# Memory rows handed over in two parts, Q and K passes interleaved, and layernorm rows transposed by DMA in a two-layer attention kernel

## The chip, the cores and the metric

The kernel runs on one core of one Trainium2 chip, as one launch. The metric is device time in microseconds, smaller is better. Before the change three runs took 2330.82, 2334.03 and 2334.85 us; the median is 2334.03. The profiled execution has a span of 2335.8 us.

## The reference

Four layers are applied in turn to x of 2048 tokens by 640 features: A, B, A, B. Each adds its output to x, and each gets the layernorm of x as input. A is a linear and softmax attention with 32 heads of 20 in four segments; the change leaves it alone. B is a recurrence over 64 segments of 32 tokens:

```
mem = mem0                                    # 8 memory rows of 640
for s in range(64):
    h = concat(mem, xs)                       # 8 + 32 rows
    q, k, v = h @ Wq, h @ Wk, h @ Wv          # 32 heads of 128
    p = softmax(mask(q k^T / sqrt(128)))
    o = (p v) @ Wo
    mem, out[s] = o[:8], o[8:]
```

The memory rows of a step are the first eight output rows of the step before. So a step can begin to project its memory only when the output projection of the step before is done.

## The kernel before

Everything is in bfloat16 with float32 sums. Only layer B is touched. The order of the instructions on TensorE (PE), ScalarE (ACT), VectorE (DVE) and GpSimd (POOL) is the order of the program text, held by explicit order edges; the DMAs that SP issues are not in those edges.

**A step of layer B** (the loop from line 933, `i4` = s mod 4, `T` = s // 4) works on 32 new columns: 8 memory rows and 24 tokens of the next segment, all in the transposed tile `hT[s]` of 128 partitions by 5 chunks by 56 columns. Columns 24 to 32 are the memory. The last 8 tokens of each of four segments (a group T) are collected in `hx[T]` by `tail_cols` (line 776), a POOL copy, and are projected by "tail" units, which serve as filling work of the steps i4 = 1, 2, 3 of the group before. In i4 = 0 the filling work is the output projection of the group's 32 deferred rows (`b_OPSd`).

**A pass** (`thin_parts`, line 750) is five parts, one for each chunk c of 128 features. A part is four matmuls of 32 output rows by 512 columns that share the array; it adds into one PSUM buffer of a pool of three. The tile names are `b_Qa`, `b_Ka`, `b_Qb`, `b_Kb` (Q and K of heads 0 to 15 and 16 to 31) and `b_V`. When a Q or K pass ends (`QKPass`, line 1002), DVE turns the 32x32 blocks of its sums (`turn`, into `b_TQ`, two buffers), DVE casts the memory columns into `QT[s]` or `KT[s]`, and POOL casts the other 24 for step s + 1.

**The order of a step** on PE: Qa, Ka, Qb, two parts of Kb, `scores(0)`, three parts of Kb, then, if there are any, the transposes of `ln_tr`; one part of V0, `sums(0)`, four parts of V0, `scores(1)`, three parts of V1, `values(0)`, two parts of V1, `sums(1)`, half of the output projection `b_OPS`, filling work, `values(1)`, more filling work, the other half of `b_OPS`, and by `fill(9)` all the filling work that is left.

**The hand-over** (lines 1157 to 1162): when `b_OPS` is done, DVE turns all 320 columns of it into `b_TM` by one stream transpose, and two adds of 64 partitions by 40 elements write the memory columns of `hT[s + 1]`. PE meanwhile works on what `fill(9)` issued; then its first weight load of Qa waits for those columns.

**The layernorm for layer B** goes by groups of 128 tokens. In the steps with i4 = 2, `ln_norm` and `ln_apply` make the normed rows `b_xn` (one buffer, DVE). In the next step, `ln_tr` (line 710) transposes its five blocks on PE into PSUM, and ACT copies them to `b_xnTg`, a tile of two buffers. Its readers are POOL copies: `tail_cols` one step later, and `alloc_h` from three steps later on. At a layer's start group 1 is made just before the loop and transposed in step 0; there SP also loads the second part of the output weights `b_wo` (line 915).

**SP's queue** in a step carries the loads of the residual rows (`b_XO`, line 1120, `b_XOd`, line 929), the stores of the results (lines 1172 and 1185) and, every four steps, the load of the next 128 rows (`b_xt`, line 698).

Of the kernel before, what the change touches and what calls it, by code (L numbers as in the profile page):

```python
# [19 lines left out]
BF16 = mybir.dt.bfloat16  # L20
ACT = mybir.ActivationFunctionType
ALU = mybir.AluOpType
# [7 lines left out]
NCH = 5  # L30
# [630 lines left out]
def layer_B(nc, nc_raw, tc, C, W, br, outer, wo_src, x_src, xb_src, x_dst, general, nsteps=64, out_bf16=False):  # L661
# [3 lines left out]
    NT = nsteps // 4  # L665
    with ExitStack() as ctx:
# [38 lines left out]
        def ln_apply(g):  # L705
            xt, (mv, rstd) = ln_n[g]
            xn = ln_n[g] = wk.tile([128, D], BF16, name="b_xn", tag="xn")
            layernorm_apply(nc, xt[:], xn[:], mv, rstd)

        def ln_tr(g):  # L710
            xn = ln_n.pop(g)
            tps = pot.tile([128, NCH, 128], BF16, name="b_lntps", tag="ot")
            for c in range(NCH):
                nc.tensor.transpose(tps[:, c, :], xn[:, 128 * c:128 * c + 128], C.identb[:])
            xg = wk2.tile([128, NCH, 128], BF16, name="b_xnTg")
            nc.scalar.copy(xg[:], tps[:])
            xnT_g[g] = xg

        def xcols(s, a, b):
# [4 lines left out]
        hT, QT, KT = {}, {}, {}  # L724
# [51 lines left out]
        def tail_cols(T):  # L776
            if T not in hx:
                hx[T] = wk.tile([128, NCH, 32], BF16, name="b_hx", tag="hx")
                v = xnT_g[T][:].rearrange("p c (i t) -> p c i t", t=32)[:, :, :, 24:32]
                nc.gpsimd.tensor_copy(hx[T][:].rearrange("p c (i t) -> p c i t", t=8), v)  # L780
            return lambda c: hx[T][:, c, :]
# [135 lines left out]
        pot = ctx.enter_context(tc.tile_pool(name="b_pot", bufs=2, reuse_waits="tile", space=PSUM))  # L917
# [15 lines left out]
        for s in range(nsteps):  # L933
            last = (s == nsteps - 1)
            T, i4 = divmod(s, 4)
# [20 lines left out]
            def fill(us):  # L956

                while queue and us > 0.1:
                    cost, f = queue.pop(0)
                    f()  # L960
                    us -= cost
# [56 lines left out]
            def qk(Wt, name, b, dst):  # L1018

                QKPass(Wt, name, b, dst).run()  # L1020
# [36 lines left out]
            def normalise(b):  # L1057

                R = (wk if general else sm).tile([128, 4, 40], F32, name="b_R", tag="R")
                flat = R[:].rearrange("p r c -> p (r c)")  # L1060
                nc.scalar.activation(out=flat, in_=SP[b][:, 256:416], func=ACT.Ln)
                nc.scalar.activation(out=flat, in_=flat, func=ACT.Exp, scale=-1.0)
                nc.vector.tensor_tensor(out=PT[:, b, :, 16:56], in0=PT[:, b, :, 16:56], in1=R[:], op=ALU.mult)
                nc.gpsimd.tensor_tensor(out=PT[:, b, :, 0:16], in0=PT[:, b, :, 0:16], in1=R[:, :, 24:40], op=ALU.mult)
                if not general:
                    nc.gpsimd.tensor_tensor(out=Rtot[:], in0=Rtot[:], in1=R[:], op=ALU.add)
# [13 lines left out]
            def take(eng, b, jp):  # L1080
                h = 16 * b + 8 * jp
                evac(eng, OTsb[:, h:h + 8, :].rearrange("p (j r) c -> p j (r c)", j=2), OTL[b, jp][:, :, 0:160])
# [11 lines left out]
                    if not self.parts:  # L1094
                        evac(("act", "dve")[self.b], Vsb[:, self.b, :], self.ps[:])

            qk(W.wq, "b_Qa", 0, QT)
            qk(W.wk, "b_Ka", 0, KT)
            qk(W.wq, "b_Qb", 1, QT)
            if general:  # L1100
                row_max(0)
# [3 lines left out]
            K1.run(3)  # L1105
            while xn_pending:
                ln_tr(xn_pending.pop(0))
            if i4 == 0 and T + 1 < NT:
                tail_cols(T + 1)
            V0 = VPass(0)  # L1110
            V0.run(1)
            sums(0)
# [17 lines left out]
            take("act", 0, 0)  # L1130
            take("act", 0, 1)
            normalise(1)
            if g_need < NT:
                ln_apply(g_need)
                xn_pending.append(g_need)
            if i4 != 3:
                tails_to_seg(s + 1)
            op = OPass(lambda h: OTsb[:, h, 0:32], HORDER, "b_OPS", po, "op")
# [9 lines left out]
            ops = op.ps  # L1148
# [7 lines left out]
                deferred[T] = OPass(lambda h, t_=OTd: t_[:, h, :], HORDER, "b_OPSd")  # L1156
            if not last:
                TM = wk.tile([128, 10, 32], F32, name="b_TM", tag="TM")
                nc.vector.transpose(out=TM[:].rearrange("p g t -> p (g t)"), in_=ops[:])
                for hf in range(2):  # L1160
                    nc.vector.tensor_tensor(out=hT[s + 1][64 * hf:64 * hf + 64, :, 24:32], in0=TM[0:64, hf:10:2, 24:32],
                                            in1=TM[64:128, hf:10:2, 24:32], op=ALU.add)
            fill(9)
            flush()
            if not last and i4 == 3:
# [36 lines left out]
def full_kernel(tc, A_x, A_wq, A_wk, A_wv, A_wo, A_beta, B_x, B_mem0, B_Wq, B_Wk, B_Wv, B_Wo, B_seg_len, out, layers="ABAB"):  # L1202
    nc = tc.nc
    with ExitStack() as ctx:
# [14 lines left out]
        def run(general):  # L1219
            nc.scalar.preload_act_table_set("natural_log_exp_and_others")  # L1220
            nl = len(layers)
            assert layers == "AB" * (nl // 2)
            onc = _OrdNC(tc, nc, engines=ORDER_ENGINES)
            for li in range(0, nl, 2):
                lastl = (li == nl - 2)
                first = li == 0 and not general
                with ExitStack() as bridge, ExitStack() as outer:
                    outer.bridge = bridge
                    br = layer_A(onc, nc, tc, C, WA, A_wv, A_wo, xin if li == 0 else X, X, Xb, li == 0, general, outer, mem0,
                                 prep=prep if first else None, prefetch=loads if first else ())  # L1230
                    layer_B(onc, nc, tc, C, WB, br, outer, wo_src, X, Xb, xout if lastl else X, general, out_bf16=lastl)
# [61 lines left out]
```

## Time and profile before

| what | value |
|---|---|
| span of the profiled execution | 2335.8 us |
| PE busy | 2225.5 us, 95% |
| DVE busy | 1576.3 us, 67% |
| POOL busy | 1036.7 us, 44% |
| ACT busy | 950.3 us, 41% |
| transpose b_TM, 128x320 | 126 times, 517 ns |
| add into b_hT, 64x40 | 252 times, 195 ns at least |
| transposes b_lntps, 128x128 | 150 times, 219 ns (median) |
| copy b_xnTg | 30 times, 692 ns |
| copy b_hx | 30 times, 407 ns (median) |

A row of the timeline gives the start in us from the span's start, the duration in us, the engine, the operation with the tile written and the tiles read, the shape, the count of merged instructions, and in brackets the idle time of the engine just before with what ended it. PEld is the weight load, which runs ahead of the matmuls. A row of the waits gives the total in us, the number of waits and the longest. A row of the chain gives start and duration of a piece of the path that ended last. The matmuls' ends are modelled, and four of a part run side by side, so lengths are better taken from starts. The page's first line of each engine counts busy time, its share of the span, and instructions.

Layer B takes two stretches of the span, from about 317 to 1150 us and from about 1476 to 2326 us. A step of it lasts 12.95 to 13.5 us.

### The profile page before, as it was taken

How to read it: one execution, taken by the hardware profiler on the slowest of the kernel's cores; microseconds unless marked ns; L12 is line 12 of the kernel's file. 1: busy time of each engine (PE TensorE's matmuls, PEld its weight loads, DVE VectorE, ACT ScalarE, POOL GpSimd, SP SyncE). 2: the span in 40 equal slices, each digit the busy share in tenths (PEclk: the TensorE clock that was granted, in tenths of full speed). 3: DMA queues.
4: the chain of work that ended last, by engine and by line, in shares of the span. 5: the costliest groups of instructions: out<-in, count | busy, mean ns of one | idle time of the engine just before them, and what ended most of it. 6: DMA issues, size and time to landing. Idle time of an engine off the chain costs nothing.

```text
span 2335.8 us, 122651 instructions
## 1 busy us (share of the span) xinstructions
PE 2225.5 (95%) x54988; PEld 1238.1 (53%) x54988; DVE 1576.3 (67%) x3618; ACT 950.3 (41%) x2207; POOL 1036.7 (44%) x2475
## 2 busy tenths in 40 slices
PE   6999989999999999999889899899999999999997
PEld 3444545555555555555545445455555555555554
DVE  5777746666666666666657777566666666666664
ACT  5776823323232333323257767223333233323332
POOL 3344534444444444444324445344444444444442
PEclk9999989999999999999989999999999999999998
DMA  6555540000000000000133334300000000000000
GB/s 165 146 148 152 161 142 20 21 18 20 18 19 19 20 21 20 21 15 17 31 104 115 108 117 127 124 18 15 17 15 17 16 18 16 17 18 16 14 12 14
DMA packets 90649, 123.38 MB, mean 53 GB/s; under 512 B 16496, under 2 KB 80000, under 8 KB 88192
## 3 DMA queue, kind: packets, MB, share of 16 engines
q1 hardware_dynamic: 87648, 111.84, 16.9%
q8 instruction: 431, 7.06, 1.3%
q10 hardware_dynamic: 2464, 3.61, 0.6%
q14 instruction: 106, 0.87, 0.1%
HBM read 89.17 MB, written 26.21 MB: 49 GB/s over the span
## 4 chain that ended last, share of the span: by engine, by line
PE 80%; DVE 10%; ACT 5%; issue 2%; DMA 2%; POOL 0%; SPq 0%; DVEq 0%; ACTq 0%; POOLq 0%
PE b_OPS L85 14%; PE b_V L85 13%; PE b_Qa L85 7%; PE b_tail L85 7%; PE b_Kb L85 6%; PE b_Ka L85 6%; PE b_Qb L85 6%; PE b_SP L85 4%; PE a_PP L85 4%; ACT a_PT L85 4%; PE b_OTL L85 3%; PE b_OPSd L85 3%; PE a_S L85 2%; PE a_pv L85 2%; DVE a_qk L85 2%
## 5 line engine op out<-in xcount | busy, mean ns | idle before, releaser
L85 PEld LDWEIGHTS <-b_hT 128*32 128x32 bf16 x15120 | 369.8, 96 | 334.7 <-DVE b_hT L85 66.6
L85 ACT ACTIVATE b_PT<-b_SP 128x224 bf16<-128x224 f32 x256 | 92.2, 360 | 784.6 <-DVE b_TQ L85 740.2
L85 PE MATMUL b_V<-b_wv,b_hT 128*32 128x512 bf16 x5040 | 355.8, 381 | 0.0
L85 ACT ACTIVATE a_PT<-a_S 128x768 bf16<-128x768 f32 (+1 forms) x384 | 326.7, 892 | 62.4 <-PE a_S L85 56.2
L85 PE MATMUL b_OPS<-b_wo,b_OTsb 128*32 128x320 bf16 x8192 | 329.9, 303 | 6.5 <-DVE b_OTsb L85 5.2
L85 PEld LDWEIGHTS <-b_OTsb 128*32 128x32 bf16 x8192 | 197.3, 97 | 115.4 <-DVE b_OTsb L85 49.4
L85 POOL CAST b_QT<-b_TQ 128x384 bf16<-128x384 f32 x254 | 142.7, 562 | 240.9 <-DVE b_TQ L85 240.9
L85 ACT CAST b_OTsb<-b_OTL 128x320 bf16<-128x320 f32 x384 | 151.0, 428 | 232.3 <-PE b_OTL L85 204.7
L85 POOL CAST b_KT<-b_TQ 128x384 bf16<-128x384 f32 x254 | 142.9, 563 | 175.5 <-DVE b_TQ L85 174.3
L85 POOL TENSOR_TENSOR b_PT<-b_PT,b_R 128x64 bf16<-128x64 bf16 x256 | 105.6, 412 | 222.1 <-ACT b_R L85 197.4
L85 POOL TENSOR_SCALAR_AFFINE_SELECT a_PT<-a_PT 128x256 bf16<-128x256 bf16 x256 | 109.0, 427 | 172.6 <-ACT a_PT L85 161.0
L85 PE MATMUL b_Kb<-b_wk,b_hT 128*32 128x512 bf16 x2520 | 182.5, 380 | 0.0
L85 PE MATMUL b_Qa<-b_wq,b_hT 128*32 128x512 bf16 x2520 | 162.3, 387 | 13.7 <-DVE b_hT L85 7.2
L85 PE MATMUL b_Ka<-b_wk,b_hT 128*32 128x512 bf16 x2520 | 160.0, 383 | 0.0
L85 PE MATMUL b_Qb<-b_wq,b_hT 128*32 128x512 bf16 x2520 | 158.1, 380 | 0.0
L85 PE MATMUL a_PP<-a_xnT,a_wt 128*128 128x512 bf16 x560 | 146.1, 394 | 5.2 <-DVE a_um L85 1.5
L85 DVE STREAM_TRANSPOSE b_TM<-b_OPS 128x320 f32<-128x320 f32 x126 | 65.1, 517 | 118.2 <-PE b_OPS L85 118.2
L85 PE MATMUL a_S<-a_qk 32*128 32x512 bf16 (+3 forms) x1024 | 137.3, 308 | 7.8 <-ACT a_PT L85 6.5
L85 DVE CAST b_Vsb<-b_V 128x512 bf16<-128x512 f32 x128 | 88.5, 692 | 74.6 <-PE b_SP L85 43.9
L85 DVE TENSOR_TENSOR b_PT<-b_PT,b_R 128x160 bf16<-128x160 bf16 x256 | 103.8, 405 | 48.3 <-ACT b_R L85 29.2
L85 DVE STREAM_TRANSPOSE b_TQ<-b_Qa 128x512 f32<-128x512 f32 x128 | 91.7, 717 | 65.7 <-PE b_Qa L85 45.4
L85 DVE CAST b_OTsb<-b_OTL 128x320 bf16<-128x320 f32 x128 | 62.9, 492 | 106.0 <-PE b_OTL L85 105.2
(165 smaller groups left out, 4270.0 us busy)
## 6 DMA issues: line engine op xcount, KB each, us to landing
a_wt<-a_wpad SPq DMA_DIRECT2D x112, 160.0 KB
b_XO<-xres SPq DMA_DIRECT2D x256, 30.0 KB
a_wvo<-in_A_wo_dram SPq DMA_DIRECT2D x8, 800.0 KB
b_wq<-in_B_Wq_dram SPq DMA_DIRECT2D x20, 256.0 KB
b_wk<-in_B_Wk_dram SPq DMA_DIRECT2D x20, 256.0 KB
xres<-a_xo SPq DMA_DIRECT2D x16, 320.0 KB
xres_bf<-a_xb SPq DMA_DIRECT2D x32, 160.0 KB
b_wv<-in_B_Wv_dram SPq DMA_DIRECT2D x20, 256.0 KB
```

The costliest lines, as they stand in the source:

```text
L85: r = f(*a, **k)
```

## The change

There are four edits.

1. The hand-over is made in two parts: DVE turns the first 128 columns of `b_OPS` (chunks 0 and 1) and adds them into `hT[s + 1]`, then the other 192 (chunks 2 to 4).
2. The passes Qa and Ka are interleaved: two parts of Q, two of K, three of Q, three of K. So chunks 2 to 4 are first read by the fifth part.
3. `tail_cols(T + 1)`, in steps with i4 = 0, moves from behind the Kb pass to behind `normalise(1)`.
4. `ln_tr` issues one transposing DMA on SP's queue, from `b_xn` to `b_xnTg` in SBUF, in the place of five PE transposes, their PSUM tile and the ACT copy.

```diff
         def ln_tr(g):
             xn = ln_n.pop(g)
-            tps = pot.tile([128, NCH, 128], BF16, name="b_lntps", tag="ot")
-            for c in range(NCH):
-                nc.tensor.transpose(tps[:, c, :], xn[:, 128 * c:128 * c + 128], C.identb[:])
             xg = wk2.tile([128, NCH, 128], BF16, name="b_xnTg")
-            nc.scalar.copy(xg[:], tps[:])
+            nc.sync.dma_start(xg[:], xn[:], transpose=True)
             xnT_g[g] = xg
...
-            qk(W.wq, "b_Qa", 0, QT)
-            qk(W.wk, "b_Ka", 0, KT)
+            Q0, K0 = QKPass(W.wq, "b_Qa", 0, QT), QKPass(W.wk, "b_Ka", 0, KT)
+            Q0.run(2)
+            K0.run(2)
+            Q0.run(3)
+            K0.run(3)
             qk(W.wq, "b_Qb", 1, QT)
...
             while xn_pending:
                 ln_tr(xn_pending.pop(0))
-            if i4 == 0 and T + 1 < NT:
-                tail_cols(T + 1)
             V0 = VPass(0)
...
             normalise(1)
+            if i4 == 0 and T + 1 < NT:
+                tail_cols(T + 1)
             if g_need < NT:
...
                 TM = wk.tile([128, 10, 32], F32, name="b_TM", tag="TM")
-                nc.vector.transpose(out=TM[:].rearrange("p g t -> p (g t)"), in_=ops[:])
-                for hf in range(2):
-                    nc.vector.tensor_tensor(out=hT[s + 1][64 * hf:64 * hf + 64, :, 24:32], in0=TM[0:64, hf:10:2, 24:32],
-                                            in1=TM[64:128, hf:10:2, 24:32], op=ALU.add)
+                for c0, c1 in ((0, 2), (2, NCH)):
+                    nc.vector.transpose(out=TM[:, 2 * c0:2 * c1].rearrange("p g t -> p (g t)"), in_=ops[:, 64 * c0:64 * c1])
+                    for hf in range(2):
+                        nc.vector.tensor_tensor(out=hT[s + 1][64 * hf:64 * hf + 64, c0:c1, 24:32], in0=TM[0:64, 2 * c0 + hf:2 * c1:2, 24:32],
+                                                in1=TM[64:128, 2 * c0 + hf:2 * c1:2, 24:32], op=ALU.add)
```

## The prediction

> **What bounds the kernel now.** I read the page's busy shares and its chain first.
>
> ```profile
> PE 2225.5 (95%) x54988; PEld 1238.1 (53%) x54988; DVE 1576.3 (67%) x3618; ACT 950.3 (41%) x2207; POOL 1036.7 (44%) x2475
> PE 80%; DVE 10%; ACT 5%; issue 2%; DMA 2%; POOL 0%; SPq 0%; DVEq 0%; ACTq 0%; POOLq 0%
> ```
>
> TensorE is the bound; DVE has a tenth of the chain, and in layer B that tenth is chiefly the hand-over between steps. So only what shortens TensorE's queue, or a wait of TensorE, is worth time. Second, the waits of TensorE's weight loads:
>
> ```profile
> PEld L85 <- DVE b_hT L85: 66.6, 126, 1.7
> PEld L85 <- DVE b_xn L85: 11.9, 28, 0.4
> ```
>
> Each of the 126 hand-overs waits for the memory rows in b_hT. Part of it is only the loader running ahead of the array, so third, the timeline at one hand-over (i4 = 2 to 3):
>
> ```profile
> 729.12 1.25 PE L85 MATMUL b_tail<-b_wq,b_hx 128*32 128x512 bf16 x20
> 729.34 0.52 DVE L85 STREAM_TRANSPOSE b_TM<-b_OPS 128x320 f32<-128x320 f32 x1 [0.44 <-PE b_OPS L85]
> 729.89 0.53 DVE L85 TENSOR_TENSOR b_hT<-b_TM 64x40 bf16<-64x40 f32 x2
> 730.46 0.72 DVE L85 STREAM_TRANSPOSE b_TQ<-b_tail 128x512 f32<-128x512 f32 x1
> 730.48 2.06 PEld L85 LDWEIGHTS <-b_hT 128*32 128x32 bf16 x44 [0.61 <-DVE b_hT L85]
> 731.87 0.72 DVE L85 STREAM_TRANSPOSE b_TQ<-b_Qa 128x512 f32<-128x512 f32 x1 [0.69 <-POOL b_QTt L85]
> ```
>
> Call x the start of the b_TM transpose (729.34). In the chain, 20 such matmuls are spaced 1.08 us, 0.2155 us per part of four. The tail fill would therefore let Qa start at 729.12 + 1.08 = 730.20, x + 0.86; it starts at 730.48, x + 1.14. The array loses 0.28 us, not 0.61. By the same sum the hand-over after i4 = 1 loses 0.18 (fill from 716.16, Qa at 717.42), that after i4 = 3 loses 0.28, and that after i4 = 0, filled by nine b_OPSd parts of 0.135 from 703.21, loses 0.05. A group of four steps loses 0.79 us.
>
> Fourth, the chain through a step with the layernorm transposes and one without:
>
> ```profile
> 721.56 0.67 PE b_Kb L85 x12
> 722.24 0.22 PE b_V L85 x4
> ...
> 734.63 0.67 PE b_Kb L85 x12
> 735.30 0.39 PE b_lntps L85 x5
> 735.68 0.33 PE b_V L85 x4
> ```
>
> The five transposes take 0.39 us on the bounding engine, and the first V part after them 0.11 more.
>
> **What the Trainium skill says.** "TensorE: Matmul & The Clock Gate", Back-to-back issue gap, gives N/2.4 + 2.5 ns for warm matmuls: 215.8 ns at 512 columns. The trace agrees (0.2155). "VectorE: DVE Perf Modes", The three transpose paths, prices a crossbar DMA transpose of a 128x128 bf16 block at 1309 ns; no transfer of this trace is one. "DMA: Bandwidth & Descriptors", Queues, rings and completion order, says that descriptors are consumed in ring order; the trace cannot show it, but it decides where a transpose behind a large load lands.
>
> **Rows turned in two parts.** DVE transposes of 512 and 320 columns last 717 and 517 ns: 1.04 ns a column and 184 fixed. So 128 columns cost 0.317 and 192 cost 0.384 us. The two adds last 195 ns at 40 elements, some 0.17 at 16 and 0.18 at 24. The first half is ready at x + 0.317 + 0.03 + 0.17 + 0.03 + 0.17 + 0.05 (semaphore) = x + 0.77. After i4 = 2 and 3 POOL's b_OTdef copy overlaps and the adds take 0.53 instead of 0.43, so I take x + 0.87. The array is free at x + 0.85, so the hand-overs gain 0.05, 0.17, 0.25 and 0.25: 0.72 a group. The second half follows after 0.414 + 0.42, at x + 1.60 to 1.75.
>
> **Q and K interleaved.** Q0 and K0 run two parts each before Q0 needs chunk 2: 4 x 0.2155 = 0.86 us after a start at x + 0.86, so x + 1.72. The second half is just in time; its price lies between 0 and 0.1 a step, and I take 0. The price elsewhere is that the Q pass ends two parts later, counting from its start t0 (6 x 0.2155 + 0.38 = 1.67 us), and K only three parts after it. DVE must turn Q and K back to back. What this takes is seen at the start of the layer:
>
> ```profile
> 317.81 0.71 DVE L85 STREAM_TRANSPOSE b_TQ<-b_Qa 128x512 f32<-128x512 f32 x1
> 318.55 0.23 DVE L85 CAST b_QT<-b_TQ 128x128 bf16<-128x128 f32 x1
> 318.69 0.71 DVE L85 STREAM_TRANSPOSE b_TQ<-b_Ka 128x512 f32<-128x512 f32 x1
> 319.44 0.23 DVE L85 CAST b_KT<-b_TQ 128x128 bf16<-128x128 f32 x1
> ```
>
> A turn and its cast recur every 0.88 us. So Q's turn starts at t0 + 1.67 + 0.12 = 1.79, K's at 2.67, and K's cast ends at 3.65 (before: Qa at 704.46, cast end at 707.91, 3.45). scores(0) loads K at 708.14, t0 + 3.68. With 0.05 of semaphore the stall is 0.02 to 0.06 us; if cast and turn did not overlap (0.98 apart) it would be 0.12. I take 0.04 a step, 0.16 a group. Queued behind the longer b_TM chain (DVE ends at x + 1.6 instead of 0.98) are the second tail turn or add_out: 0.72 or 1.01, done by x + 2.6, while Q's turn is wanted at x + 2.65. PSUM slots hold: scores(0) takes Ka's, free at t0 + 3.39.
>
> Sum: 0.72 - 0.16 = 0.56 a group, times 15 filled groups in each of two layers: 16.8 us. The six hand-overs without fill (start and end of the layers) gain about 0.25 each, 1.5. Together 18.
>
> **Layernorm transposes by DMA.** Removed: 30 times five TensorE transposes. A step with them lasts 742.83 - 729.34 = 13.49 us, one without 12.95, of which 0.10 is the larger loss at the hand-over it begins with: 0.44, times 30 = 13 us. The ACT copy (692 ns x30) also goes, at no gain: ACT is busy for 41%. Added: 30 transposes on SP's queue. b_xn is ready at 726.94; its first reader is the b_hx copy of the next i4 = 0 step, now behind normalise(1) at about 753.7. That is 26 us, against 5 x 1.31 = 6.5 us (an estimate from the skill's price) and SP behind it: the next store waits for DVE until 738.29 anyway. So it costs nothing in the steady state; the work that hides it is a whole step of matmuls. Bounds: 0 to the rival below. At a layer's start the transpose shares SP with the b_wo loads (issued at 318.53), on which layer two's chain waits 12.94 us. Behind them it lands when DMA falls quiet near 331, plus some us, and POOL has until about 336 (its cast of step 1's Q starts at 338.11, and the b_QT, c_tot, b_OTdef and b_hT copies between take 1.5); ahead of them it delays them by its length. Between 0 and 6.5 us a layer; I take 0.5, 1 in all.
>
> **tail_cols moved.** One POOL copy of 0.40 us, x30, passes values(0)'s b_PT multiply; the chain shows no loss there (OTL follows V at 750.98 as elsewhere) and POOL's next piece, the b_QT copy, is needed 7 us later. Nothing. It issues no DMA.
>
> **Total:** 18 + 13 - 1 = 30 us off the profiled span of 2335.8. The unprofiled runs are 2330.8 to 2334.9, so 2334 - 30 = 2304.
>
> **Rivals.**
> Hand-over paid back: the second half comes 0.1 late in every step (12 us of 120 filled hand-overs), or the K turn costs 0.12 instead of 0.04 (10 us), or both. Speaks for it: both margins are below 0.1 us. One of them leaves 18 to 20 us, both leave 8: 2314 to 2326, most likely 2316.
> No early release: if TensorE's first weight load waits for all four adds, it starts at x + 1.60 instead of x + 1.03 to 1.14, 0.5 x 126 = 63 slower, less 13: 2384. Against it: scores(0) reads half of QT (708.14) before the cast into its other half (708.76), so waits go by region.
> The other side, by DMA: at both layer starts, with DMA share over 1, TensorE stops for an unnamed reason, in the chain
>
> ```profile
> 323.65 3.19 issue
> ```
>
> (2.65 us in layer two), which looks like starved instruction supply. If each transpose did that, 30 x 3 = 90 us less 31 gained: near 2393. It decides from 31/30, 1.0 us, a transpose. Against it: the 160 KB b_xt load at 726.96 leaves no gap on TensorE.
> No change: half of the hand-over gain is lost and layer starts cost 6 us each with some stalls; about 2332.
>
> **How the numbers follow.** Forecast 0.56 (2290 to 2313); paid back 0.22; no early release 0.06; starved by DMA 0.09; no change 0.07. Within 0.2% (4.7 us, about what a measurement here can tell) is no change. Faster: 0.56 + 0.22 less a little = 0.77; slower 0.06 + 0.09 + 0.01 = 0.16. Range 2288 to 2331: the first two cases.
>
> **What would show it.** Right: b_TM as x252 at about 0.32 and 0.38 us; the b_hT wait down from 66.6 to some 45 us or less; b_Ka starting 0.43 after b_Qa; no b_lntps, i4 = 3 steps at 13.0 us; b_hx never waiting for a DMA. Wrong: new waits of scores(0) on b_KT above 0.06 a step, of b_Qa on the second add, "issue" gaps on TensorE beside the transposes, or POOL stopped at b_hx early in a layer.

## The result and the profile after

| kernel | median us | range | runs | ratio to before (95% interval) |
|---|---|---|---|---|
| before | 2333.35 | 2330.82 to 2334.85 | 4 | |
| changed | 2313.88 | 2309.95 to 2317.14 | 4 | 0.9917 [0.9899, 0.9935] |

The change makes the kernel 0.8% faster, 19.5 us where 30 were forecast. The profiled span fell from 2335.8 to 2315.4 us. That run is the slowest of the four, so sums over the trace may come out a few us off the medians.

The busy shares and the chain of the changed kernel:

```profile
PE 2201.0 (95%) x54838; PEld 1238.7 (53%) x54838; DVE 1629.0 (70%) x3996; ACT 931.9 (40%) x2177; POOL 1025.8 (44%) x2475
PE 79%; DVE 9%; ACT 5%; DMA 3%; issue 2%; SPq 1%; POOL 0%; DVEq 0%; ACTq 0%; POOLq 0%
```

TensorE still sets the time. Its busy time fell by 24.5 us and its instruction count by 150, the `b_lntps` transposes. DVE works 53 us more and its part of the chain is smaller. New in the chain is SP's queue (1%), and DMA has 3% instead of 2%: a first hint of where the rest went.

The hand-over from i4 = 2 to 3, in the timeline. It answers to the one shown before, and x is again the start of the first `b_TM` transpose (721.75):

```profile
721.52 1.25 PE L85 MATMUL b_tail<-b_wq,b_hx 128*32 128x512 bf16 x20
721.75 0.32 DVE L85 STREAM_TRANSPOSE b_TM<-b_OPS 128x128 f32<-128x128 f32 x1 [0.44 <-PE b_OPS L85]
722.10 0.47 DVE L85 TENSOR_TENSOR b_hT<-b_TM 64x16 bf16<-64x16 f32 x2
722.60 0.38 DVE L85 STREAM_TRANSPOSE b_TM<-b_OPS 128x192 f32<-128x192 f32 x1
722.62 0.62 PE L85 MATMUL b_Qa<-b_wq,b_hT 128*32 128x512 bf16 x8
723.02 0.39 DVE L85 TENSOR_TENSOR b_hT<-b_TM 64x24 bf16<-64x24 f32 x2
723.07 0.61 PE L85 MATMUL b_Ka<-b_wk,b_hT 128*32 128x512 bf16 x8
723.50 0.82 PE L85 MATMUL b_Qa<-b_wq,b_hT 128*32 128x512 bf16 x12
724.44 0.72 DVE L85 STREAM_TRANSPOSE b_TQ<-b_Qa 128x512 f32<-128x512 f32 x1 [0.28 <-PE b_Qa L85]
```

The tail fill would let Qa start at 721.52 + 1.08 = 722.60; it starts at 722.62. The loss is 0.02 us where it was 0.28. The second half is complete at 723.41 (x + 1.66), and the part that reads it runs from 723.50: just in time, with nothing to spare beyond the hand-over to the weight load. It holds not only here: in 121 of the 126 hand-overs the third part of Q starts 0.86 to 0.88 us after the first, which is four parts of 0.2155. (Three others take 0.91 or 0.92 us, and the first of each layer 1.68, where TensorE's clock is halved; more on that below.) The same steps in the chain show that nothing else is lost there:

```profile
721.69 1.08 PE b_tail L85 x20
722.77 0.47 PE b_Qa L85 x8
723.24 0.43 PE b_Ka L85 x8
723.67 0.65 PE b_Qa L85 x12
724.32 0.65 PE b_Ka L85 x12
```

The waits of TensorE's loader, however, did not fall:

```profile
PEld L85 <- DVE b_hT L85: 68.8, 218, 1.4
PEld L85 <- DVE b_KT L85: 40.3, 251, 0.2
```

The columns are the total, the number of waits and the longest, in us. Now there are nearly two waits to a hand-over instead of one, and each is mostly the loader standing ahead of an array that has work. Waits of PEld overstate the loss; the chain and the step lengths don't.

Step lengths (from one first `b_TM` transpose to the next, medians over the steps 4 to 59 of each layer):

| us | i4=0 | i4=1 | i4=2 | i4=3 | sum of four |
|---|---|---|---|---|---|
| before, first layer B | 13.025 | 12.958 | 12.957 | 13.489 | 52.43 |
| changed, first layer B | 12.826 | 12.913 | 12.856 | 12.796 | 51.39 |
| before, second layer B | 13.026 | 12.957 | 12.961 | 13.490 | 52.43 |
| changed, second layer B | 12.822 | 12.914 | 12.769 | 12.798 | 51.30 |

A group gains 1.04 and 1.13 us; 1.00 was forecast (0.56 + 0.44). Times 15 in each layer, 32.5 us. So the normal step does what was forecast, and about 12 us of it are lost at places that the medians don't see. The excess, which is what these steps are longer than their medians in sum (shorter ones counted against), rose from 1.32 and 1.18 us (first and second layer B) to 6.47 and 3.96. The start of a layer, from the first `b_Qa` to the first `b_TM`, takes 19.89 and 21.17 us instead of 18.89 and 19.40. What follows the last `b_TM` takes 29.89 instead of 26.84. This whole difference lies behind the last computing instruction, the cast of `c_flag`: 9.04 us remain after it instead of 5.97. In the other two kernels without the transposing DMA (e1, e9, below) it is 6.0, in the nine others with it 5.9 to 9.7. No instruction of an edit stands there, and why it differs stays open.

Three groups of waits in the changed kernel belong to these places:

```profile
PE b_OPS L85 <- DMA b_wo<-in_B_Wo_dram: 10.3, 4, 4.0
DVE b_XO L85 <- DMA b_XO<-xres: 5.3, 5, 1.8
PE b_Kb L85 <- DVE b_TQ L85: 3.2, 5, 1.3
```

Before, the first was 1.2 us (one wait), the second 4.1 (six waits, which held up little: 1.3 us of excess in that layer), the third 0.4.

The late `b_XO` is worth following once, for three steps of the first layer B (38, 46 and 54) last 14.58, 14.27 and 13.76 us. Step 38, with SP's issues ("SPq") of the step before it:

```profile
801.91 3.51 SPq L1186 DMA_DIRECT2D xres<-b_XOd  x8
806.80 2.83 SPq L926 DMA_DIRECT2D b_XOd<-xres  x5
809.70 0.82 SPq L1173 DMA_DIRECT2D xres<-b_XO  x2
810.56 1.02 SPq L926 DMA_DIRECT2D b_XOd<-xres  x3
811.69 2.14 SPq L1118 DMA_DIRECT2D b_XO<-xres  x2
815.36 1.01 DVE L85 TENSOR_TENSOR b_XO<-b_OPS,b_XO 64x320 f32<-64x320 f32 x2 [1.78 <-DMA b_XO<-xres]
816.40 0.72 DVE L85 STREAM_TRANSPOSE b_TQ<-b_Qa 128x512 f32<-128x512 f32 x1
817.17 0.62 PE L85 MATMUL b_Kb<-b_wk,b_hT 128*32 128x512 bf16 x8 [0.90 <-DVE b_TQ L85]
```

SP stores eight pieces of `b_XOd`, then reloads eight, with the store of the last `b_XO` result among them (809.70). The addition works in place, so the one `b_XO` tile can be loaded again only when that store has read it. The load (811.69) lands so late that DVE stands 1.78 us before its addition. The turn of Qa is queued behind that addition, and so TensorE stands 0.90 us before Kb: its PSUM slot is still waiting to be turned.

One more thing differs from execution to execution. The trace has stretches in which TensorE was granted half its clock, 89 us of them in this execution (95 in that of the kernel before), most of them in layers A, and one at each start of a layer B. Two of them, at the start of the first layer B of the changed kernel and of e4 below, in a view by stretches (the stretch, its length, busy time of PE, PEld, DVE, ACT and POOL, the granted clock, the busy share of DMA, GB/s):

```profile
328.50:338.70 10.20, 7.01 (x80) 2.71 (x76) 2.77 (x9) 0.42 (x1) 0.98 (x4) 0.50 0.20 68
323.80:327.20 3.40, 2.87 (x65) 1.72 (x68) 1.01 (x2) 1.40 (x4) 0.55 (x2) 0.50 1.07 363
```

So the length of a layer's start mixes waiting and clock. TensorE's idle time in it doesn't: 4.4 and 5.1 us before (first and second layer B), 6.7 and 7.5 in the changed kernel. The steps 4 to 59 meet no such stretch in any kernel here.

### The profile page after: what moved, and what is told of

It is laid out like the page before. It is cut to its first block, busy times and chain, and to the rows that moved or that the text cites. A ratio compares the mean times of both kernels' runs of the same rounds, so it can differ in the third digit from the quotient of the medians.

```text
span 2315.4 us, 122732 instructions
## 1 busy us (share of the span) xinstructions
PE 2201.0 (95%) x54838; PEld 1238.7 (53%) x54838; DVE 1629.0 (70%) x3996; ACT 931.9 (40%) x2177; POOL 1025.8 (44%) x2475
## 4 chain that ended last, share of the span: by engine, by line
PE 79%; DVE 9%; ACT 5%; DMA 3%; issue 2%; SPq 1%; POOL 0%; DVEq 0%; ACTq 0%; POOLq 0%
PE b_OPS L85 13%; PE b_V L85 12%; PE b_tail L85 9%; PE b_Qa L85 6%; PE b_Kb L85 6%; PE b_Ka L85 6%; PE b_Qb L85 5%; PE b_SP L85 4%; ACT a_PT L85 4%; PE a_PP L85 4%; PE b_OTL L85 3%; PE b_OPSd L85 3%; PE a_S L85 2%; PE a_pv L85 2%; DVE a_qk L85 2%
## 5 line engine op out<-in xcount | busy, mean ns | idle before, releaser
L85 PEld LDWEIGHTS <-b_hT 128*32 128x32 bf16 x15120 | 379.0, 96 | 306.6 <-DVE b_hT L85 68.8
L85 PE MATMUL b_Qa<-b_wq,b_hT 128*32 128x512 bf16 x2520 | 183.5, 384 | 5.0 <-DVE b_hT L85 5.0
L85 PE MATMUL b_Ka<-b_wk,b_hT 128*32 128x512 bf16 x2520 | 182.1, 382 | 0.0
L85 DVE STREAM_TRANSPOSE b_TM<-b_OPS 128x128 f32<-128x128 f32 x252 | 88.2, 350 | 126.1 <-PE b_OPS L85 122.2
L85 DVE TENSOR_TENSOR b_PT<-b_PT,b_R 128x160 bf16<-128x160 bf16 x256 | 110.1, 430 | 28.6 <-ACT b_R L85 27.0
L85 POOL TENSOR_TENSOR b_Rtot<-b_Rtot,b_R 128x160 bf16<-128x160 bf16 x256 | 126.7, 495 | 0.0
```

The source lines that it names most:

```text
L85: r = f(*a, **k)
```

## The experiments

Each was timed beside the kernel before on the same chip, in three sets: e1 to e4, e5 to e8, e9 to e11. The medians of before in them are 2331.68, 2331.55 and 2335.03 us, and the ratio is to these.

| run | median us | range | ratio (95% interval) |
|---|---|---|---|
| e1_rows_only | 2315.29 | 2311.08 to 2316.43 | 0.992 [0.9903, 0.9937] |
| e2_dma_only | 2332.73 | 2327.64 to 2337.57 | 0.9999 [0.9986, 1.0011] |
| e3_split_in_order | 2358.16 | 2355.76 to 2362.07 | 1.0109 [1.0091, 1.0127] |
| e4_first_on_pe | 2310.23 | 2308.57 to 2313.05 | 0.9906 [0.9887, 0.9926] |
| e5_two_xo | 2306.57 | 2305.13 to 2307.47 | 0.9884 [0.9866, 0.9902] |
| e6_dma_twice | 2314.87 | 2313.83 to 2321.16 | 0.9926 [0.991, 0.9942] |
| e7_shift16 | 2314.49 | 2303.61 to 2317.95 | 0.9913 [0.9893, 0.9933] |
| e8_best | 2305.36 | 2304.48 to 2310.39 | 0.989 [0.9873, 0.9908] |
| e9_pe_two_xo | 2312.99 | 2309.19 to 2316.81 | 0.9905 [0.9888, 0.9923] |
| e10_tail_back | 2309.60 | 2308.76 to 2310.76 | 0.989 [0.9873, 0.9906] |
| e11_two_xo_again | 2308.95 | 2308.55 to 2309.89 | 0.9887 [0.9871, 0.9903] |

The tiles and loops in the diffs are those of the change. Differences of 3 us between kernels lie inside the intervals of the ratios; they are read below only together with the step lengths and waits of the traces, of which there is one to a kernel.

The mean granted clock, which nearly every run has on record, goes with the times too. Over 105 runs (those of this table, of the kernel before beside them, and of the changed kernel), each taken against the mean of its kernel and set, 0.001 less clock goes with 1.4 us more time (correlation -0.71). And in each set the kernels with the transposing DMA had less of it than those without: in the first before and e1 have means of 0.984 and 0.983, e2, e3 and e4 of 0.981, 0.980 and 0.982. Whether the DMA lowers the clock is not shown.

### The rows and the interleaving alone (e1_rows_only)

Edits 1 and 2 on the kernel before:

```diff
-            qk(W.wq, "b_Qa", 0, QT)
-            qk(W.wk, "b_Ka", 0, KT)
+            Q0, K0 = QKPass(W.wq, "b_Qa", 0, QT), QKPass(W.wk, "b_Ka", 0, KT)
+            Q0.run(2)
+            K0.run(2)
+            Q0.run(3)
+            K0.run(3)
...
-                nc.vector.transpose(out=TM[:].rearrange("p g t -> p (g t)"), in_=ops[:])
...
+                for c0, c1 in ((0, 2), (2, NCH)):
+                    nc.vector.transpose(out=TM[:, 2 * c0:2 * c1].rearrange("p g t -> p (g t)"), in_=ops[:, 64 * c0:64 * c1])
...
```

> Edits 1 and 2 alone: the hand-over in two parts and the interleaved Q and K passes; layernorm transposes on PE and tail_cols at its old place. Working theory (the hand-over gives what it does in the steady steps, some 0.6 us a group, and the late loads of the residual rows come from the longer DVE chain and not from the transposing DMA): 15 to 18 us below before, near 2317, with some b_XO waits on a DMA in the i4 = 1 steps. Rival (the late loads are made by the transposing DMA on SP's queue): 18 us or more below before, and no such waits beyond those of before.

Measured: 2331.68 - 2315.29 = 16.4 us off, where the prediction's sum for these edits is 18. Step medians of the first layer B are 12.821, 12.912, 12.767 and 13.231. The `b_lntps` are still in the last, and the other three are as in the changed kernel or below. `b_wo` and `b_XO` are waited for 1.2 and 0.9 us in all, the excess over the medians is 1.21 and 1.99 us, and layer starts take 19.10 and 20.08 us (+0.2 and +0.7). So the hand-over pays almost in full, and the late loads and most of the long layer starts don't come from it: the working theory that DVE's longer chain makes the late loads falls.

### The transposing DMA alone (e2_dma_only)

Edit 4 on the kernel before:

```diff
-            tps = pot.tile([128, NCH, 128], BF16, name="b_lntps", tag="ot")
-            for c in range(NCH):
-                nc.tensor.transpose(tps[:, c, :], xn[:, 128 * c:128 * c + 128], C.identb[:])
...
-            nc.scalar.copy(xg[:], tps[:])
+            nc.sync.dma_start(xg[:], xn[:], transpose=True)
```

> Edit 4 alone: the transposes by DMA, tail_cols at its old place, hand-over and pass order as before. Working theory: 13 us less for the 30 steps with transposes, 2 to 3 us back at the two layer starts, where the transpose goes out ahead of the b_wo loads: 10 us below before, near 2323. Rival (the DMA slows SP's queue for others): 5 us or less below before, with b_XO waits on a DMA above 8 us in all. A third: tail_cols at its old place makes POOL wait for the transpose; then b_hx shows waits on a DMA.

Measured: no gain in the time, as the rival with its `b_XO` waits above 8 us had it. The i4=3 step did fall, from 13.489 to 13.055 us, by the 0.43 of the prediction; 30 of them are 13 us. A large part is given back in the waits of this kernel:

```profile
PE b_OPS L85 <- DMA b_wo<-in_B_Wo_dram: 11.2, 4, 4.7
DVE b_XO L85 <- DMA b_XO<-xres: 9.6, 7, 2.5
```

Layer starts take 20.07 and 21.55 us (+1.2 and +2.2), the excess over the medians is 5.56 and 2.03 us (+5.1 in all). From the first to the last hand-over the two layers together are 7.5 us shorter than before, not 13. The two losses come with the transposing DMA, without the other edits. They leave a gain of some 4 us, which the times don't show. The clock can account for that: the 14 runs have a mean of 0.0031 less than before, worth some 4 us by the slope above (an estimate).

### Two parts, but Q and K in order (e3_split_in_order)

The changed kernel with the old order of the passes:

```diff
-            Q0, K0 = QKPass(W.wq, "b_Qa", 0, QT), QKPass(W.wk, "b_Ka", 0, KT)
-            Q0.run(2)
-            K0.run(2)
-            Q0.run(3)
-            K0.run(3)
+            qk(W.wq, "b_Qa", 0, QT)
+            qk(W.wk, "b_Ka", 0, KT)
```

> The changed kernel without edit 2: rows in two parts, but Qa runs whole before Ka. Chunk 2 is then wanted two parts after the start, at x + 0.86 + 0.43 = x + 1.29, and written at x + 1.60 to 1.75. If the interleaving is what covers the second half: a stall of 0.3 to 0.45 us in the Qa pass of each hand-over, so 0.5 x 126 x 0.7, some 40 us slower than the changed kernel, and slower than before by 10 to 25 (2345 to 2360). If the early start alone brings the gain and the second half isn't waited for: equal to the changed kernel, 2314.

Measured: 2358.16, 26.5 us slower than the kernel before and 44 slower than the changed one. Steps of the first layer B last 13.183, 13.293, 13.147 and 13.208, so 0.29 to 0.41 more than in the changed kernel, and the wait moved to where the second half is read:

```profile
PEld L85 <- DVE b_hT L85: 124.2, 222, 1.4
PE b_Qa L85 <- DVE b_hT L85: 30.3, 129, 0.8
```

The sum is that of the timeline above: Q's third part would start 2 x 0.2155 = 0.43 us after x + 0.87, at x + 1.30, and its rows are ready at x + 1.66. That is 0.36 us a step. Here rows in two parts are a gain only with work put between the two; alone they are a loss, for the second half lands later (x + 1.66) than Q started on the whole before (x + 1.14).

### The transposition out of the layer's start (e4_first_on_pe)

In the changed kernel SP issues the first transposition of a layer ahead of `b_wo`:

```profile
316.78 1.32 SPq L713 DMA_TRANSPOSE b_xnTg<-b_xn  x1
318.15 0.56 SPq L698 DMA_DIRECT2D b_xt<-xres_bf  x1
318.94 1.39 SPq L912 DMA_DIRECT2D b_wo<-in_B_Wo_dram  x2
327.52 0.72 PE L85 MATMUL b_OPS<-b_wo,b_OTsb 128*32 128x320 bf16 x14 [3.41 <-DMA b_wo<-in_B_Wo_dram]
331.89 1.78 PE L85 MATMUL b_OPS<-b_wo,b_OTsb 128*32 128x320 bf16 x22 [1.72 <-DMA b_wo<-in_B_Wo_dram]
```

The experiment is the changed kernel with that one group turned by TensorE:

```diff
-            nc.sync.dma_start(xg[:], xn[:], transpose=True)
+            if g == 1:
+                tps = pot.tile([128, NCH, 128], BF16, name="b_lntps", tag="ot")
+                for c in range(NCH):
+                    nc.tensor.transpose(tps[:, c, :], xn[:, 128 * c:128 * c + 128], C.identb[:])
+                nc.scalar.copy(xg[:], tps[:])
+            else:
+                nc.sync.dma_start(xg[:], xn[:], transpose=True)
```

> The changed kernel with group 1 of each layer transposed on PE and copied by ACT as before; the other 28 transposes stay on DMA. If the transpose ahead of the b_wo loads costs what the first step shows (1.0 and 1.8 us more from the first Qa to the first b_TM): 2 to 3 us below the changed kernel, b_OPS waiting for b_wo some 3 us less in all. If these waits come from elsewhere: equal to the changed kernel or 1 us slower.

Measured: 2310.23, 3.6 below the changed kernel. The starts take 17.94 and 20.02 us (19.89 and 21.17 in the changed kernel), 3.1 us less in all, and the wait for `b_wo` is 0.7 us. SP now issues `b_wo` at 316.49, 3.58 us after the first `b_Qa` instead of 5.13. TensorE's idle time in the starts, which the clock doesn't touch, is 4.3 and 4.8 us, down from 6.7 and 7.5. The run takes the transposition away from there; the DMA issued behind the loads of `b_wo` instead was not run, so the order alone is not tested. The late `b_XO` stays (6.8 us in six waits, excess 6.86 us): it is a loss of its own.

### Two b_XO tiles (e5_two_xo, e11_two_xo_again)

The changed kernel with two tiles used in turn:

```diff
-        XO = st.tile([64, 320], F32, name="b_XO")
-        nc.vector.memset(XO[:], 0.0)
+        XOs = [st.tile([64, 320], F32, name=f"b_XO{i}") for i in range(2)]
+        for XO in XOs:
+            nc.vector.memset(XO[:], 0.0)
...
+            XO = XOs[s % 2]
...
-            def store(s=s, ops=ops):
+            def store(s=s, ops=ops, XO=XO):
```

> The changed kernel with two b_XO tiles used in turn instead of one; all else as changed. Theory A: what the changed kernel loses in the first layer beside its normal steps (6.5 us above the medians, three steps of 14.58, 14.27 and 13.76 instead of 12.86) is the b_XO load landing late behind SP's stores, because the load into the one tile can't go out before the addition of the step before has read it. With two tiles the load can go out a step earlier: the waits of the addition on b_XO vanish, excess of layer 0 falls from 6.5 to 1.5 to 3, and the time is 4 to 6 us below the changed kernel, about 2309. Theory B (the transposing DMA itself holds SP or the DMA engines, whatever stands behind it): the late steps stay or turn up at another load, 2312 to 2316.

Measured: 2306.57, 7.3 below the changed kernel and 8 below e6 and e7 of the same set, which differ from the changed kernel in other things. No wait of `b_XO` for its load is left. Step 46, in the changed kernel 14.27 us long, starts here at 914.23, and its addition comes 1.60 us later, without a wait:

```profile
897.60 0.75 SPq L1120 DMA_DIRECT2D b_XO<-xres  x2
914.02 1.99 SPq L1120 DMA_DIRECT2D b_XO<-xres  x2
915.83 1.01 DVE L85 TENSOR_TENSOR b_XO<-b_OPS,b_XO 64x320 f32<-64x320 f32 x2
916.89 0.72 DVE L85 STREAM_TRANSPOSE b_TQ<-b_Qa 128x512 f32<-128x512 f32 x1
```

SP's burst is as late as before (914.02 follows it), but nobody waits: the second half of that load is issued only after the addition has begun, so the addition reads the other tile, loaded at 897.60, ahead of the burst. The excess in the first layer B fell only to 3.78 us, where 1.5 to 3 was expected, and in the second it stayed at 3.81. So something else is scattered over the steps, which e9 takes up. Nor do the tiles account for all of the gain: of the 9.7 us between the two profiled spans, 4.2 lie between the first and the last hand-over of the layers, 2.5 in the end and 3.2 before and between the layers B, where 41 us instead of 58 were at half clock. The repetition:

> The kernel with two b_XO tiles once more, unchanged, so that the two others have it beside them on the same chip: 2305 to 2308 as before; a median outside of 2303 to 2310 would mean that differences of 3 us between calls mean nothing.

Measured: 2308.95 where before is 2335.03, ratio 0.9887 against 0.9884. The same. Between the first and the last hand-over it is 5.9 us shorter than the changed kernel (e10, which also has two tiles, 4.5). So 4 to 6 us is what two tiles are worth in the steps, as expected.

### Twice the DMA (e6_dma_twice)

The changed kernel with each transposition issued once more, into a tile that nobody reads:

```diff
             nc.sync.dma_start(xg[:], xn[:], transpose=True)
+            xg2 = wk.tile([128, NCH, 128], BF16, name="b_xnTg2")
+            nc.sync.dma_start(xg2[:], xn[:], transpose=True)
```

> The changed kernel with every transposing DMA issued twice (the second one into a tile nobody reads): 30 more such DMAs, 1.23 us of SP each and some 670 packets each. Theory B (the transposing DMA is what costs, by its time on SP, its packets, or the engines' supply of instructions): at least twice the loss seen so far, so 6 us or more above the changed kernel, 2320 or more, above all at the layers' starts, where SP issues the transposition ahead of b_wo: one more there is 1.3 us a layer, 2.6 in all. Theory A (only where a late load falls): layer starts +2 to +3 in all, the rest within 4 us either way, 2312 to 2319.

Measured: 2314.87, 1.0 above the changed kernel. The layer starts grew by 1.6 and 1.3 us, as forecast for one more in front of `b_wo`; the first layer's excess grew from 6.5 to 9.6 and the second's stayed (3.70). Theory B, at least 2320, falls: from the first to the last hand-over the two layers are only 2.4 us longer. A cost in proportion to the number of these DMAs is out; one that comes with the first and doesn't grow with the second is not.

### SP's program shifted (e7_shift16)

The changed kernel with 16 loads of 64 bytes on SP's queue ahead of the first layer's steps, into a tile that nobody reads:

```diff
+        if not out_bf16:
+            pad_t = st.tile([1, 16 * 32], BF16, name="b_pad")
+            for k in range(16):
+                nc_raw.sync.dma_start(pad_t[:, 32 * k:32 * k + 32], wo_src[0:1, k, 0:32])
```

> The changed kernel with 16 tiny loads on SP (64 bytes each, into a tile nobody reads) put ahead of the first layer's steps; nothing else differs. On SP a single DMA issue of 1.0 to 1.5 us without a wait comes every 90 to 100 instructions; in the kernel before two groups are 90, so it always fell in the same place, and in the changed kernel it drifts and falls into the stores and loads of b_XO of the first layer. Theory A (this drift is what makes three loads late): with the places shifted by 16 the late steps move or vanish; excess of layer 0 falls from 6.5 to between 1 and 4, time 2 to 5 us below the changed kernel (after about 0.6 us for the 16 loads themselves, if they stand on the path). Theory B (the transposing DMA itself): the same three steps are late by the same amounts, excess 6 to 7, time as the changed kernel or 1 us above.

Measured: a miss for both theories. Late steps are 30, 46 and 54 (1.45, 1.57 and 1.74 us over the median), the excess is 7.85 us, the time 2314.49. Theory A wanted 1 to 4 us of excess, theory B the same three steps. SP's slow issues stand at the same instructions as without the shift, each 16 rows later in the count (`b_XOd` loads at rows 734, 829 and 923 instead of 718, 813 and 907). So they follow the place in the code and not a count from its beginning, and my account of a drifting period is wrong.

Set side by side, the traces of all kernels show more regularity than that. In the first layer B the steps that are over 0.6 us late, in every kernel with the DMA and one tile (e2, e3, e4, e6, e7, the changed one), are among 6, 14, 22, 30, 38, 46 and 54, which is every second group, and 46 and 54 are in all six. SP's burst falls in the step before, and there a reload of `b_XOd` is often slow to issue: in the ten kernels with the DMA 4 to 8 such reloads of the first layer B, in the steps 5, 13, 21 and so on to 61, and none in the second; in the three without it (before, e1, e9) none in the first and 7 or 8 in the second, where they did no such harm.

What the slow issues go with, the packet records show. A plain DMA issue takes SP 0.31 us in the median; 42 in the changed kernel take over 0.95. Each of the 42 ends 0.24 to 0.40 us after the end of a 16 KB packet of the instruction queue (q8, 430 packets in the span; median 0.38). In the kernel before it holds for 64 of 65. But 144 issues of under 0.40 us lie wholly inside such a packet. So SP seems to wait for certain of these packets and not for all, which would fit its own next instructions; whose they are, the records don't say. A packet of this kind can also go with a late store. From SP's waits in 905 to 925, before the late step 46:

```profile
SPq L926 <- DMA xres<-b_XOd: 2.7, 3, 2.1
```

A q8 packet runs from 910.02 to 911.23; 124 packets of the stores end by 910.56, the last four start at 911.22, and SP's reload of `b_XOd` waits for them until 912.4. In the kernel with the rows alone the same wait is 0.9 us. Of the 15 such bursts in the first layer B of the changed kernel, 12 have the store's last packet 0.70 to 0.72 us after its last issue; in the three others it is 1.46 to 1.65 us, and a q8 packet lies in each of these three. So SP's burst ends at other times from kernel to kernel and group to group, and whether a `b_XO` load comes late or not hangs on it.

### Both losses mended (e8_best)

e4 and e5 together.

> Both: the second group of each layer's normed rows transposed by the matrix engine as before (its transposition stood ahead of the b_wo loads on SP), the others by DMA, and two b_XO tiles. If the two losses found (layer start, late b_XO) are separate, their gains add: 3.6 us from the first (measured alone), 3 to 5 from the second, so 2304 to 2308, the lowest of all kernels here. If the late loads aren't mended by two tiles, 2309 to 2311, as with the first alone.

Measured: 2305.36, ratio 0.989, the lowest median here, 8.5 us below the changed kernel; but its lead over e5 is smaller than the spread of either. Layer starts are 17.94 and 19.74 us, no `b_XO` waits, excess 3.66 and 2.95 us. The gains don't add up to 11; what e5 has from the end and from layers A, above, is not shown to be a gain of its tiles. In the second layer TensorE waits 4.2 us for `b_wo` again, with no transposition ahead of it, and the start is no longer than in e4: a wait for `b_wo` alone is no measure of the loss.

### What the DMA is worth without late loads (e9_pe_two_xo), and tail_cols (e10_tail_back)

e9 is e5 with all groups turned by TensorE and copied by ACT, as before:

```diff
+            tps = pot.tile([128, NCH, 128], BF16, name="b_lntps", tag="ot")
+            for c in range(NCH):
+                nc.tensor.transpose(tps[:, c, :], xn[:, 128 * c:128 * c + 128], C.identb[:])
...
-            nc.sync.dma_start(xg[:], xn[:], transpose=True)
+            nc.scalar.copy(xg[:], tps[:])
```

> The changed kernel with two b_XO tiles, but all normed rows transposed by the matrix engine as in the kernel before: what the transposing DMA alone is worth once late b_XO loads can't eat it. Theory A (its 0.44 us in each of 30 groups is real, 13 us; its costs are the layers' starts, 2 to 3 us in all, and the late loads, now gone): 9 to 11 us above the kernel with two tiles and the DMA (2306.57 measured), so 2315 to 2318; i4=3 steps 13.23 instead of 12.80. Rival (the gain of the transposing DMA is eaten by something spread over all steps, whatever the tiles, as the run with the DMA alone and its ratio of 0.9999 suggest): at most 4 us above, 2307 to 2311.

Measured: 2312.99 against 2308.95 of e11 beside it, 4.0 us. My theory A (9 to 11) falls, the rival stands, if at its edge; e9 had 0.0012 more clock than e11, and by the slope above 4.0 would be some 6 at the same clock (an estimate), which is between the two. The i4=3 medians are 13.24 and 12.80, so the 13 us are there. Against them stand layer starts of 20.22 and 20.91 us in place of 17.99 and 19.09 (4.1 us), and the excess of 4.22 and 3.20 in place of 0.50 and 1.82 (5.1 us). That leaves 4. About half of the new excess (2.6 us) is TensorE standing still, for no wait that the profile names, in the runs of small matmuls of `values(0)`, as here in e11:

```profile
819.72 0.20 PE L85 MATMUL b_OTL<-b_PT,b_Vsb 32*128 32x40 bf16 x4
820.33 0.19 PE L85 MATMUL b_OTL<-b_PT,b_Vtb 32*128 32x16 bf16 x4 [0.36 <-issue]
```

The gaps before `b_OTL` in steps 4 to 59 of both layers sum to 3.1 us in e11, 3.8 and 4.5 in e5 and e10 and 2.4 in e8; in e9, e1 and the kernel before, without the DMA, to 0.5, 0.25 and 1.0. With the DMA and one tile they are 2.3 in the changed kernel and e6, 2.0 in e4, but 1.3, 1.0 and 0.5 in e2, e7 and e3. So the DMA doesn't always bring them, and what does is not settled.

e10 is e5 with `tail_cols` in its old place:

```diff
             while xn_pending:
                 ln_tr(xn_pending.pop(0))
+            if i4 == 0 and T + 1 < NT:
+                tail_cols(T + 1)
...
             normalise(1)
-            if i4 == 0 and T + 1 < NT:
-                tail_cols(T + 1)
```

> The changed kernel with two b_XO tiles, tail_cols back in its old place behind the K pass of head half b; all else the same. The prediction put the move of tail_cols at nothing. If so: i4=0 steps 12.82 to 12.84 as with the move, and a time within 2 us of the kernel with two tiles (2306.57). If the move matters, it shows in the i4=0 steps alone (tail_cols runs only there, 15 times a layer): 0.1 us a step would be 3 us.

Measured: 2309.60 against 2308.95, and i4=0 medians of 12.830 and 12.825 against 12.832 and 12.829. The move does nothing, as the prediction had it.

## Why the prediction was right, and where it was not

**The direction and the range were right; one term, the DMA's, was taken too high.** Of the forecast 30 us, 19.5 came. That the range held is partly luck: its upper half was drawn for a hand-over that is paid back, which didn't happen, and the largest of the losses that did happen, the late loads, was in neither.

- **Rows in two parts, Q and K interleaved, 18 us:** right. Alone they give 16.4. Its parts hold too: Qa at x + 0.87 (forecast 0.87), the second half at x + 1.66 (1.60 to 1.75), Q's turn 1.82 us after Q's start (1.79), K's at 2.72 (2.67), scores(0) reading K 3.74 after it (it was 3.68: 0.06 a step, where 0.04 was taken). The price of just in time, taken as 0, is 0.01 us or less in 121 of 126 hand-overs.
- **Layernorm transposes by DMA, 13 us:** the 0.44 of a step is right (0.43 alone, 0.44 in e9 against e11), but the clause "So it costs nothing in the steady state" failed. It asked only whether the transposition lands in time for `b_hx`, which it does by far, and whether SP is free. It did not ask how much room the other loads on SP's queue have: with one `b_XO` tile, the load behind the `b_XOd` burst lands just before it is wanted. Kernels with the DMA and one tile (e2, e3, e4, e6, e7, the changed one) wait there for 5.3 to 9.6 us in five to seven waits; of those without it e1 waits for 0.9 and the kernel before for 4.1, which held up little. What often goes with the late burst is a slow reload of `b_XOd`: the first layer B has them in every kernel with the DMA and in none without. The step from the DMA to these is not closed: its own time on SP is not it (e6), nor the place in SP's count (e7), and what remains is that the instruction packets fall elsewhere. In all the DMA made the two layers 7.5 to 7.7 us shorter between the first and the last hand-over (e2 against before, e11 against e9), and 4.4 with one tile and the rows in two parts (the changed kernel against e1), where 13 were forecast.
- **Layer starts, 1 us:** too small, within the bounds given. "Ahead of them it delays them by its length" is what happened: counted from the first `b_Qa`, `b_wo` is issued 1.55 and 2.00 us later than before, and the starts of the changed kernel are 1.0 and 1.8 us longer, with 2.3 us more idle time of TensorE in each. The prediction left open which comes first; the code decides that, for `ln_tr` of the first group stands ahead of the loads of `b_wo`.
- **tail_cols moved, nothing:** right (e10).
- **Of the signs,** `b_TM` x252 at 0.32 and 0.38, `b_Ka` 0.45 us after `b_Qa`, no `b_lntps`, and `b_hx` without a wait came true. "The b_hT wait down from 66.6 to some 45" did not: the reading of that wait was wrong, as it counts a loader that is ahead, twice a step now. i4 = 3 at 13.0 was 12.80: 13.49 - 0.44 - 0.25 was at hand.
- **The rivals.** The time is at the lower edge of "hand-over paid back" (2314 to 2326), but its mechanism isn't there: neither margin broke. "Starved by DMA" is out in its size: the unnamed stalls of TensorE at `b_OTL` are 0.5 to 4.5 us in all with the DMA instead of 90, and that they come from it is not shown. "No early release" is out: Qa starts before the second turn ends.

The 11 us that are missing are, in the two profiled executions, the starts of two layers (2.8), more scattered delays (7.9), and a longer end (3.1), against 2.7 more from the steps than forecast (32.5 against 29.8). The end lies behind the last computing instruction, and its cause is open. That the first two come with the transposing DMA is shown by e2 and e9; that the transposition ahead of `b_wo` makes the most of the first, by e4. That the single `b_XO` tile lets part of the second through to TensorE is shown by e5 and e11: with two tiles the excess is 2.8 and 3.0 us less, of the 7.9, and the steps are 4 to 6 us shorter in all. What TensorE waits for before `b_OTL`, and why the granted clock differs between the kernels, stays open.

## What to carry to other kernels

When a result is handed on in parts, put into the consumer's queue as much other work as lies between the parts' arrivals; without it the split was a loss here, 44 us between two orders of the same instructions. When work moves from the bounding engine to a DMA queue, look not only at its own deadline but at every load issued behind it, and give those that go out just in time a second buffer: one tile of 80 KB here was worth 4 to 6 us in the steps, beside 19.5 of the whole change. Judge a wait of the weight loader by the chain and by the length of a step, not by its total. And before small differences between kernels are read, compare the granted clock of their runs and where in the traces the differences lie.

## What the runs showed of the hardware

- A transposing DMA of 128x640 bf16 holds SP for 1.23 us (median of 30) and, in a quiet stretch, its last packet ends 2.13 us after the issue begins: 640 packets of 256 bytes, all within 1.19 to 2.12 us, and 32 of 4 bytes. The Trainium skill, "VectorE: DVE Perf Modes", The three transpose paths, has 1309 ns for a single 128x128 block, from which I had estimated 6.5 us for five blocks. The measurement decides for this tile: a third of that.
- SP's plain DMA issues of 0.95 us and more, 42 of 42 in the changed kernel, end 0.24 to 0.40 us after a 16 KB packet of the instruction queue; and the last four packets of one store came 0.66 us after the others (910.56 to 911.22), just as such a packet (910.02 to 911.23) ended.
- In the start of the first layer B the kernel before shows 3.19 us of unnamed standstill and nearly no wait for `b_wo`; the changed kernel 0.30 us of it, and 3.41 and 1.72 us of waiting for `b_wo`; in e4 it is 2.72 and 0.24 again. The one stands in the place of the other, and why is not shown.
- TensorE's granted clock is 0.50 in 89 us of the changed kernel's execution (10.2 us of it at the start of the first layer B, 3.4 there in e4), and over 105 runs 0.001 less mean clock goes with 1.4 us more time.
